# The first two chunks of a linear-attention loop in another order: the second chunk's scores in banks of their own

## The chip, the cores and the metric

The kernel runs on one core of one Trainium2 chip. A core has five engines that each work through their own list of instructions in the written order: TensorE (PE, matrix products; its weight loads are shown apart as PEld), VectorE (DVE), ScalarE (ACT), GpSimd (POOL) and SyncE (SP, which here only issues transfers). They meet through semaphores. PE writes its products to PSUM, a memory of eight banks, and DVE and ACT read them there. The metric is the device time of one launch in microseconds (us), the median of three runs.

## The reference, cut to what matters

The first half is a recurrence over 768 steps for 4 sequences and 8 heads of 48 features; the second sends every token to one of 8 experts.

```
for t in range(S):
    cur = einsum('bhd,bhe->bhde', u * kt, vt)
    y[:, :, t] = einsum('bhd,bhde->bhe', rt, state + cur)
    state = w * state + einsum('bhd,bhe->bhde', kt, vt)
...
expert_idx = argmax(x @ w_gate, axis=1)
...
h = maximum(einsum('ecd,edf->ecf', disp, w1), 0.0)
y = einsum('ecf,efd->ecd', h, w2)
```

## The kernel before, in words

The recurrence is cut into 24 chunks of 128 steps, 6 for each of the 4 sequences. Inside a chunk it becomes matrix products with powers of the decay folded into the keys and queries. Then come routing, scattering of rows by expert, gathering, and the two layers of the experts. The order of everything is written by hand: the tile framework sets waits, and each engine's list follows the program text.

The work of chunk i, by the functions that the change and the prediction name:

- `prep_keys(i)` (L512, DVE) multiplies the loaded tile `dm` by the decay factors `ft`. `product(i)` (L496, on DVE or, by default, POOL) makes `P`, the product of queries and keys of the same step.
- `mix(...)` (L81 and L83, PE) sums two things into one bank `c`: the bonus of a coming chunk out of its `P`, and the gate logits of an earlier chunk out of its output `xs`. `mixed` (L88, ACT) copies that to `ct`; `pull` (L93, PE) turns it, and L94 (DVE) copies the result to `bon` or `l`. `bonus(i)` is pull and copy for the first chunks.
- `diag(i)` (L507, ACT; L505 where half of it is given to DVE) writes the bonus on the diagonal of `s`, eight blocks of 128x128.
- `scores(i)` (L526, PE) makes the products of keys and queries in a PSUM tile `a` of two banks, of which there is one. `masks(i)` (L530, DVE) copies `a` into `s` where the mask allows, so the next scores wait for the mask copy to release `a`.
- `prep_values(i)` (L518, DVE) makes `kt`; `update(i)` (L538, PE) makes the chunk's addition to the state in bank `u`; `state_of(i)` (L545 for the first chunk of a sequence, L548 for the others, DVE) makes the new state `snb`.
- `values1(i)` (L560, PE) and `values2(i)` (L569, PE) sum the output in two banks with the tag `y`: state times queries, then values times `s`. L573 (ACT) copies them to `xs`. `turn` (L105, PE) and `keep_rows` (L111, L112, ACT) turn `xs` into rows for the scatter.
- `setup_keys` (L416 on PE, L417 on ACT) makes `kk` once; its PSUM tile `gp` has the tag `lg`. `warm(n)` (L464) is n matrix products of zeros that nobody reads.

PSUM is full: one bank each for the tags `a1` (the tile `c`), `u`, `xp` and `lg`, two for `y`, two for `a`. The banks of `xp` and `lg` are used later in the loop, by `turn` and by the routing.

Ahead of the loop stand chunk 0's keys, scores and bonus and chunk 1's keys and bonus. Step i of the loop then runs scores(i+1), keys and product of chunk i+3, the mix for chunk i+2, update(i), masks(i+1), pull, turn, state, values of chunk i, diag(i+2). Step 0 and step 1 are written apart from the rest. Loads of `dm` and `bd` run five chunks ahead on SP's queue, with six buffers each.

Of the kernel before, what the change touches and what calls it, by code (L numbers as in the profile page):

```python
# [6 lines left out]
F32 = mybir.dt.float32  # L7
# [14 lines left out]
NP = H // 2  # L22
# [13 lines left out]
def rwkv_moe(nc, tc, dmj, rkv, bdc, wv, wu, uv, wg, w1, w2, out, cap):  # L36
# [4 lines left out]
    with ExitStack() as ctx:  # L41
# [175 lines left out]
        with ExitStack() as mc:  # L217
# [4 lines left out]
            ps1 = mc.enter_context(tc.tile_pool(name="ps1", bufs=1, space=PSUM))  # L222
# [188 lines left out]
                    nc.scalar.mul(out=wd[:, p], in_=idn, mul=w128[:, p:p + 1])  # L411

            def setup_keys(sps):
                gp = sps.tile([128, NP, 128], F32, tag="lg", name="gp")
                for p in range(NP):
                    nc.tensor.matmul(gp[:, p], lhsT=ft[:, p], rhs=wd[:, p], start=True, stop=True)  # L416
                nc.scalar.copy(out=kk.rearrange("q (p h) d -> q p h d", p=NP), in_=gp.rearrange("q p (h d) -> q p h d", h=2)[:, :, :, 0:D])  # L417
# [43 lines left out]
            def warm(n):  # L461
                t = ps1.tile([128, 512], F32, tag="y", name=f"warm{n}", bufs=2)
                for _ in range(n):
                    nc.tensor.matmul(t, lhsT=wz[:, 0:128], rhs=wz, start=True, stop=True)  # L464
# [33 lines left out]
            def diag(i, ps=range(NP), vector=False):  # L498
                t = T[i]
                s = t["s"] = sb[i % 3]  # L500
                for p in ps:
                    for h in range(2):
                        bon = t["bon"][:, 2 * p + h:2 * p + h + 1]
                        if vector:
                            nc.vector.tensor_scalar(out=s[:, h, p], in0=eye, scalar1=bon, scalar2=None, op0=ALU.mult)  # L505
                        else:
                            nc.scalar.mul(out=s[:, h, p], in_=eye, mul=bon)  # L507

            def prep_keys(i):
                dm = T[i]["dm"]  # L510
                n = 64 + D
                nc.vector.tensor_tensor(out=dm[:n], in0=dm[:n], in1=ft[:n].unsqueeze(1).broadcast_to([n, 2, NP, 128]), op=ALU.mult)  # L512
# [6 lines left out]

            def scores(i):  # L520
                t = T[i]
                a = t["a"] = psB.tile([128, 2, NP, 128], F32, tag="a", name=f"a{i}")
                for p in range(NP):
                    for h in range(2):
                        r = slice(64 * h, 64 * h + D)
                        nc.tensor.matmul(a[:, h, p], lhsT=t["dm"][r, 1, p], rhs=t["dm"][r, 0, p], start=True, stop=True)  # L526

            def masks(i):
                t = T[i]
                nc.vector.copy_predicated(t["s"].rearrange("q h p j -> q (h p) j"), msk.unsqueeze(1).broadcast_to([128, 8, 128]),  # L530
                                          t.pop("a").rearrange("q h p j -> q (h p) j"))

# [44 lines left out]
            def bonus(i, c, ct):  # L577
                T[i]["bon"] = sm.tile([128, 2 * E], F32, tag="bon", name=f"bon{i}")
                pull(c, ct, T[i]["bon"])
# [24 lines left out]
            c = mix(T[0]["P"], None, ps1)  # L604
            ct = mixed(c, wk)
            prep_keys(1)
            bonus(0, c, ct)
            diag(0, (0, 1))
            diag(0, (2, 3), True)
            setup_keys(ps1)  # L610
            warm(3)
            product(1, nc.vector)
            c = mix(T[1]["P"], None, ps1)
            masks(0)
            ct = mixed(c, wk)
            warm(2)
            bonus(1, c, ct)
            prep_keys(2)
            product(2, nc.vector)
            diag(1)  # L620
            ws = wstream(0, PLAN0, True)
            for i in range(NI):
                if i + 5 < NI:
                    load(i + 5)
                    load_rows(i + 5)
                if i == 0:
                    values1(0)
                    values2(0)
                    scores(1)
                    c = mix(T[2]["P"], None, ps1)  # L630
                    ct = mixed(c, wk)
                    prep_keys(3)
                    product(3)
                    masks(1)
                    bonus(2, c, ct)
                    warm(3)
                    prep_values(0)
                    prep_values(1)
                    diag(2)
                    next(ws)  # L640
                    continue
                if i == 1:
                    scores(2)
                    update(0)
                    state_of(0)
                    state["s"] = state["next"]
                    prep_values(2)
                if i > 1:
                    each(scores, i + 1)
                each(prep_keys, i + 3)  # L650
                each(product, i + 3)
                if i in (20, 21):
                    gather(0, [i - 20])
                else:
                    scatters(1)
                c = mix(T[i + 2]["P"] if i + 2 < NI else None, T[i - 1]["xs"], ps1)
                ct = mixed(c, wk)
                update(i)
                each(masks, i + 1)
                if i == NI - 1:  # L660
                    pa.close()
                    psA = mc.enter_context(tc.tile_pool(name="psA", bufs=2, space=PSUM))
                    acts = [xtrans(0, j) for j in range(3)]
                if i % NC == NC - 1:
                    xp = turn(i - 1, T[i - 1]["xs"], ps1)
                to = place_of(i - 1, sm, rows_of)
                pull(c, ct, to)
                if i + 2 < NI:
                    T[i + 2]["bon"] = to
                if i % NC < NC - 1:  # L670
                    xp = turn(i - 1, T[i - 1]["xs"], ps1)
                advance()
                next(ws)
                each(prep_values, i + 2)
                if i == NI - 1:
                    take(0)
                    for f in acts:
                        f()
                state_of(i)
                values1(i)  # L680
                each(diag, i + 2, (0, 1, 2))
                values2(i)
                each(diag, i + 2, (3,))
                keep_rows(i - 1, xp, rows_of)
                state["s"] = state.get("next")
                rout(i - 1, sm, ps1, rows_of, "rows")
                advance()
                if i == NI - 1:
                    advance()
                if i == 1:  # L690
                    setup_ok(wc)
                if i == 18:
                    early_places(sm, ps1)
                if i in (9, 13):
                    nc.gpsimd.memset(xg[i == 13], 0.0)
                T.pop(i - 1)
# [303 lines left out]
```

## Time and profile before

| what | before |
|---|---|
| median of 3 runs | 387.28 us (386.78 to 387.33) |
| the profiled execution, its own time | 386.67 us |
| its span, first to last instruction | 385.0 us |
| PE busy | 370.3 us (96%) |
| DVE busy | 236.5 us (61%) |
| ACT busy | 204.4 us (53%) |
| POOL busy | 143.9 us (37%) |

The span leaves out 1.67 us of the profiled execution's own time. The chunks run until about 130 us, the experts after that. A busy share is a mean over both, so a question on the first chunks is answered by the instructions in order of time and by windows, not by this table.

### The profile page before, as it was taken

The numbers are of one execution on the slowest core, as the hardware profiler recorded it, in microseconds if no ns is written. First come the engines' busy times: TensorE is split into PE (matmuls) and PEld (weight loads), VectorE is DVE, ScalarE is ACT, GpSimd is POOL, SyncE is SP. The second block draws the span as 40 slices with busy tenths as digits, with TensorE's granted clock in tenths as the row PEclk, the third lists the DMA queues.
The fourth block names the chain that finished last, engine by engine and source line by source line (L and its number), as shares of the span: only waits on it lengthen the run. The fifth ranks groups of instructions, "written<-read, shape, count | busy, mean of one in ns | idle before, by whom it ended". The sixth has DMA issues, their size and how long they took to land.

```text
span 385.0 us, 9378 instructions
## 1 busy us (share of the span) xinstructions
PE 370.3 (96%) x3569; PEld 335.3 (87%) x3570; DVE 236.5 (61%) x589; ACT 204.4 (53%) x565; POOL 143.9 (37%) x200
## 2 busy tenths in 40 slices
PE   8899999999999997999999999999999999999993
PEld 3677888787787887999999999999999999999992
DVE  6898899999996565736536636536536546543210
ACT  3668898788787532717427517426425525523201
POOL 7124668686662427304403403503502602202203
PEclk9999999999999998999999999999999999999998
DMA  7848868888712544744635535634733743400102
GB/s 296 340 140 289 277 241 286 272 297 263 263 39 79 190 138 130 214 134 132 177 109 163 180 109 137 205 112 120 226 111 115 207 131 113 126 3 17 43 3 72
DMA packets 20950, 62.51 MB, mean 162 GB/s; under 512 B 3996, under 2 KB 4132, under 8 KB 20896
## 3 DMA queue, kind: packets, MB, share of 16 engines
q1 hardware_dynamic: 15120, 46.74, 38.3%
q0 software_dynamic: 5632, 14.56, 11.4%
q8 instruction: 30, 0.49, 0.5%
q10 hardware_dynamic: 144, 0.52, 0.3%
q14 instruction: 24, 0.20, 0.2%
HBM read 52.58 MB, written 10.03 MB: 163 GB/s over the span
## 4 chain that ended last, share of the span: by engine, by line
PE 46%; issue 12%; POOL 2%; DMA 1%; POOLq 1%; ACT 0%; DVE 0%; ACTq 0%
PE a L318 8%; PE a L317 7%; PE a L319 7%; PE b L334 7%; PE b L335 7%; PE b L336 7%; PE yp L350 2%; POOL out L342 2%; PE tp L300 2%; DMA xg<-xsd,pidx 1%; POOLq L757 0%; DMA xsd<-xr,slot 0%; POOLq L933 0%; DVE ws L251 0%; ACT ws L250 0%
## 5 line engine op out<-in xcount | busy, mean ns | idle before, releaser
L342 POOL DMA_INDIRECT out<-yo,ids x32 | 32.4, 1014 | 162.1 <-ACT yo L341 161.1
L317 PE MATMUL a<-xh,ws 128*128 128x416 f32 (+1 forms) x216 | 75.6, 350 | 0.1
L322 ACT ACTIVATE hh<-a 128x416 fp32r<-128x416 f32 (+1 forms) x72 | 34.6, 481 | 76.1 <-PE a L319 70.7
L318 PE MATMUL a<-xl,ws 128*128 128x416 f32 (+1 forms) x216 | 72.8, 337 | 0.0
L319 PE MATMUL a<-xh,ws 128*128 128x416 f32 (+1 forms) x216 | 72.7, 336 | 0.0
L334 PE MATMUL b<-hh,ws 128*128 128x416 f32 (+2 forms) x208 | 71.4, 343 | 0.0
L323 DVE SCALAR_TENSOR_TENSOR hl<-a,hh 128x416 fp32r<-128x416 f32 (+1 forms) x72 | 39.1, 543 | 50.2 <-ACT hh L322 37.2
L336 PE MATMUL b<-hh,ws 128*128 128x416 f32 (+2 forms) x208 | 69.5, 334 | 0.0
L335 PE MATMUL b<-hl,ws 128*128 128x416 f32 (+2 forms) x208 | 69.4, 334 | 0.0
L251 DVE TENSOR_TENSOR ws<-wr,ws 128x384 fp32r<-128x384 f32 (+1 forms) x112 | 67.7, 622 | 0.6
L507 ACT ACTIVATE s<-eye,l 128x128 f32<-128x128 f32 x168 | 53.8, 392 | 15.3 <-DVE l L94 14.7
L250 ACT CAST ws<-wr 128x384 fp32r<-128x384 f32 (+1 forms) x112 | 59.9, 557 | 2.1 <-DMA xsd<-xr,slot 2.1
L337 DVE COPY yt<-b 128x416 f32<-128x416 f32 (+2 forms) x26 | 14.2, 546 | 67.2 <-PE b L336 67.2
L496 POOL TENSOR_TENSOR P<-dm 112x512 f32<-112x512 f32 x21 | 27.1, 1292 | 40.6 <-DVE dm L512 10.9
L317 PEld LDWEIGHTS a<-xh,ws 128*128 128x128 f32 x216 | 41.5, 192 | 0.9 <-DVE xl L305 0.3
L319 PEld LDWEIGHTS a<-xh,ws 128*128 128x128 f32 x216 | 41.5, 192 | 0.4
L318 PEld LDWEIGHTS a<-xl,ws 128*128 128x128 f32 x216 | 41.6, 192 | 0.3 <-DVE xl L305 0.2
L275 POOL DMA_INDIRECT xg<-xsd,pidx x32 | 35.8, 1120 | 14.1 <-issue 12.0
L334 PEld LDWEIGHTS b<-hh,ws 128*128 128x128 f32 x208 | 39.4, 190 | 0.1
L336 PEld LDWEIGHTS b<-hh,ws 128*128 128x128 f32 x208 | 39.2, 188 | 0.3
L335 PEld LDWEIGHTS b<-hl,ws 128*128 128x128 f32 x208 | 39.3, 189 | 0.0
L304 ACT CAST xh<-tp 128x416 fp32r<-128x416 f32 (+1 forms) x27 | 12.3, 472 | 47.3 <-PE tp L300 47.3
(144 smaller groups left out, 573.9 us busy)
## 6 DMA issues: line engine op xcount, KB each, us to landing
wr<-w SPq DMA_DIRECT2D x24, 512.0 KB
wr<-w SPq DMA_DIRECT2D x32, 384.0 KB
dm<-dmj SPq DMA_DIRECT2D x23, 512.0 KB
bd<-bdc SPq DMA_DIRECT2D x24, 384.0 KB
dm<-dmj ACTq DMA_DIRECT2D x1, 512.0 KB
xg<-xsd,pidx POOLq DMA_INDIRECT x32
out<-yo,ids POOLq DMA_INDIRECT x32
xsd<-xr,slot POOLq DMA_INDIRECT x24
```

The source lines that it names most:

```text
L250: nc.scalar.copy(out=hi, in_=r)
L251: low.append(lambda: nc.vector.tensor_tensor(out=lo, in0=r, in1=hi.bitcast(F32), op=ALU.subtract))
L275: nc.gpsimd.indirect_dma_start(out=xg[k % 2][:, i].bitcast(I32), out_offset=None, in_=xsd[:, :], in_offset=bass.IndirectOffsetOnAxis(ap=pi ...
L317: nc.tensor.matmul(a, lhsT=wh, rhs=xh[:, d, o], start=d == 0, stop=False)
L318: nc.tensor.matmul(a, lhsT=wh, rhs=xl[:, d, o], start=False, stop=False)
L319: nc.tensor.matmul(a, lhsT=wl, rhs=xh[:, d, o], start=False, stop=d == 2)
L323: nc.vector.scalar_tensor_tensor(out=hl[:, f, o], in0=a, scalar=0.0, in1=hh[:, f, o].bitcast(F32), op0=ALU.max, op1=ALU.subtract)
L334: nc.tensor.matmul(y, lhsT=wh, rhs=hh[:, f, o], start=f == 0, stop=False)
L335: nc.tensor.matmul(y, lhsT=wh, rhs=hl[:, f, o], start=False, stop=False)
L336: nc.tensor.matmul(y, lhsT=wl, rhs=hh[:, f, o], start=False, stop=f == 7)
L342: r = nc.gpsimd.indirect_dma_start(out=out[:, :], out_offset=bass.IndirectOffsetOnAxis(ap=ids[k][0][:qo, i:i + 1], axis=0), in_=yo, in_off ...
L507: nc.scalar.mul(out=s[:, h, p], in_=eye, mul=bon)
```

## The change

Chunk 1's scores no longer wait for the tile `a`: they go, with the two heads of a pair in different banks, to the two free banks with the tags `xp` and `lg`, straight behind chunk 0's pull. Its mask copy becomes two copies of half the size. `gp` moves to a `y` bank. Chunk 1's product stands ahead of chunk 0's bonus copy; chunk 2's keys stand ahead of chunk 0's mask. The calls of `warm` ahead of the first values are 4 in one call for 3 and 2 before; the 3 in step 0 stay, at another place. Step 0 now also holds update(0), scores(2), the state after chunk 0, and the values of chunk 1, and chunk 3's product is made by DVE and not by POOL. Step 1 leaves out what step 0 has taken over.

```diff
-                gp = sps.tile([128, NP, 128], F32, tag="lg", name="gp")
+                gp = sps.tile([128, NP, 128], F32, tag="y", name="gp", bufs=2)
...
             def scores(i):
                 t = T[i]
-                a = t["a"] = psB.tile([128, 2, NP, 128], F32, tag="a", name=f"a{i}")
+                if i == 1:
+                    a = t["a"] = [ps1.tile([128, NP, 128], F32, tag=n, name=f"a1{n}") for n in ("xp", "lg")]
+                else:
+                    a = t["a"] = psB.tile([128, 2, NP, 128], F32, tag="a", name=f"a{i}")
...
             def masks(i):
                 t = T[i]
+                if i == 1:
+                    for h, a in enumerate(t.pop("a")):
+                        nc.vector.copy_predicated(t["s"][:, h], msk.unsqueeze(1).broadcast_to([128, NP, 128]), a)
+                    return
...
             prep_keys(1)
+            product(1, nc.vector)
             bonus(0, c, ct)
+            scores(1)
             diag(0, (0, 1))
             diag(0, (2, 3), True)
+            c = mix(T[1]["P"], None, ps1)
+            ct = mixed(c, wk)
+            prep_keys(2)
             setup_keys(ps1)
-            warm(3)
-            product(1, nc.vector)
-            c = mix(T[1]["P"], None, ps1)
+            bonus(1, c, ct)
             masks(0)
-            ct = mixed(c, wk)
-            warm(2)
-            bonus(1, c, ct)
-            prep_keys(2)
+            diag(1)
             product(2, nc.vector)
-            diag(1)
+            warm(4)
+            prep_values(0)
...
                 if i == 0:
                     values1(0)
                     values2(0)
-                    scores(1)
+                    update(0)
+                    scores(2)
                     c = mix(T[2]["P"], None, ps1)
                     ct = mixed(c, wk)
+                    masks(1)
+                    state_of(0)
+                    state["s"] = state["next"]
+                    prep_values(1)
+                    warm(3)
+                    bonus(2, c, ct)
                     prep_keys(3)
-                    product(3)
-                    masks(1)
-                    bonus(2, c, ct)
-                    warm(3)
-                    prep_values(0)
-                    prep_values(1)
+                    product(3, nc.vector)
                     diag(2)
+                    values1(1)
+                    values2(1)
+                    prep_values(2)
                     next(ws)
                     continue
-                if i == 1:
-                    scores(2)
-                    update(0)
-                    state_of(0)
-                    state["s"] = state["next"]
-                    prep_values(2)
...
-                values1(i)
+                if i > 1:
+                    values1(i)
                 each(diag, i + 2, (0, 1, 2))
-                values2(i)
+                if i > 1:
+                    values2(i)
```

Below are three places of the engines' lists. A row gives line, operation, output and inputs; in a name the digit behind the letters is the chunk (`dm2` is chunk 2's tile), or for `s` and `snb` the buffer, or for `l` the group of two chunks; the number behind the underscore is the program's own.

DVE's list before, from chunk 1's keys to chunk 2's keys:

```order
L512 TENSOR_TENSOR dm1_115<-dm1_115,ft_128 112x1024
L94 COPY bon0_290<-c_282 128x16
L505 TENSOR_SCALAR s0_120<-eye_131,bon0_290 128x128 x4
L496 TENSOR_TENSOR P1_311<-dm1_115 112x512
L530 COPY_PREDICATED s0_120<-msk_130,a0_273 128x1024
L94 COPY bon1_324<-c_313 128x16
L512 TENSOR_TENSOR dm2_116<-dm2_116,ft_128 112x1024
L496 TENSOR_TENSOR P2_328<-dm2_116 112x512
```

and the same part of the list of the change, on to the first chunk's state:

```order
L496 TENSOR_TENSOR P1_290<-dm1_115 112x512
L94 COPY bon0_292<-c_282 128x16
L505 TENSOR_SCALAR s0_120<-eye_131,bon0_292 128x128 x4
L512 TENSOR_TENSOR dm2_116<-dm2_116,ft_128 112x1024
L94 COPY bon1_327<-c_313 128x16
L537 COPY_PREDICATED s0_120<-msk_130,a0_273 128x1024
L496 TENSOR_TENSOR P2_339<-dm2_116 112x512
L518 TENSOR_TENSOR kt0_346<-bd0_183,kk_129 128x384
L535 COPY_PREDICATED s1_121<-msk_130,a1xp_295 128x512
L535 COPY_PREDICATED s1_121<-msk_130,a1lg_296 128x512
L552 COPY snb0_126<-u_138 128x4x48
```

Chunk 1's product has moved ahead of the first bonus copy, chunk 2's keys ahead of the first mask copy, and the first mask copy behind the second bonus copy.

DVE's list before, from the bonus of chunk 2 to the copy that holds chunk 3's bonus (`l0`):

```order
L94 COPY bon2_382<-c_371 128x16
L518 TENSOR_TENSOR kt0_389<-bd0_183,kk_129 128x384
L518 TENSOR_TENSOR kt1_391<-bd1_185,kk_129 128x384
L545 COPY snb0_126<-u_138 128x4x48
L518 TENSOR_TENSOR kt2_422<-bd2_188,kk_129 128x384
L512 TENSOR_TENSOR dm4_118<-dm4_118,ft_128 112x1024
L530 COPY_PREDICATED s2_122<-msk_130,a2_404 128x1024
L94 COPY l0_447<-c_427 128x16
```

and in the change:

```order
L94 COPY bon2_405<-c_389 128x16
L512 TENSOR_TENSOR dm3_117<-dm3_117,ft_128 112x1024
L496 TENSOR_TENSOR P3_409<-dm3_117 112x512
L518 TENSOR_TENSOR kt2_440<-bd2_188,kk_129 128x384
L512 TENSOR_TENSOR dm4_118<-dm4_118,ft_128 112x1024
L537 COPY_PREDICATED s2_122<-msk_130,a2_380 128x1024
L94 COPY l0_468<-c_448 128x16
```

Two of the three `kt` copies and the state copy have left this stretch to the front; chunk 3's keys and its product, which POOL made before, have come into it.

ACT's list before, from chunk 2's diagonal to the `ct` of chunk 4:

```order
L507 ACTIVATE s2_122<-eye_131,bon2_382 128x128 x8
L88 COPY ct_436<-c_427 128x128
L507 ACTIVATE s0_120<-eye_131,l0_447 128x128 x6
L573 COPY xs1_485<-y1_0_461 128x2x128
L573 COPY xs1_485<-y1_1_462 128x2x128
L507 ACTIVATE s0_120<-eye_131,l0_447 128x128 x2
L111 COPY xr0_123<-idf_70 128x2
L112 COPY xr0_123<-xp0_450 128x384
L88 COPY ct_521<-c_512 128x128
```

and in the change:

```order
L507 ACTIVATE s2_122<-eye_131,bon2_405 128x128 x8
L580 COPY xs1_437<-y1_0_419 128x2x128
L580 COPY xs1_437<-y1_1_420 128x2x128
L88 COPY ct_457<-c_448 128x128
L507 ACTIVATE s0_120<-eye_131,l0_468 128x128 x8
L111 COPY xr0_123<-idf_70 128x2
L112 COPY xr0_123<-xp0_471 128x384
L88 COPY ct_521<-c_512 128x128
```

The two copies of chunk 1's output have moved ahead of chunk 3's diagonal, which before they stood in the middle of.

## Rows read from the trace of the kernel before

**Rows 1.** The profile page: the span, and each engine's busy time.

```profile
span 385.0 us, 9378 instructions
...
PE 370.3 (96%) x3569; PEld 335.3 (87%) x3570; DVE 236.5 (61%) x589; ACT 204.4 (53%) x565; POOL 143.9 (37%) x200
```

**Rows 2.** Windows: stretch, length, busy time of each engine, granted clock, DMA share, GB/s.

```profile
23.10:29.08 5.98, 5.32 (x89) 3.96 (x87) 5.52 (x19) 5.12 (x19) 1.28 (x1) 1.00 0.46 156
29.08:33.81 4.73, 4.73 (x92) 3.89 (x90) 4.52 (x16) 3.77 (x14) 1.64 (x3) 1.00 0.85 283
29.08:119.40 90.32, 89.72 (x1619) 71.97 (x1617) 82.98 (x233) 74.54 (x257) 58.65 (x59) 1.00 0.71 240
143.60:150.42 6.82, 4.78 (x38) 4.06 (x37) 3.96 (x19) 1.30 (x4) 5.60 (x5) 1.00 0.44 132
150.42:153.84 3.42, 3.42 (x18) 3.42 (x18) 2.08 (x4) 1.70 (x4) 2.51 (x4) 0.50 0.34 102
```

**Rows 3.** Timeline of DVE, 8 to 14 us: start, length, instruction, idle before and releaser.

```profile
8.11 1.22 DVE L512 TENSOR_TENSOR dm<-dm,ft 112x1024 f32<-112x1024 f32 x1
10.32 0.17 DVE L94 COPY bon<-c 128x16 f32<-128x16 f32 x1 [0.99 <-PE c L93]
...
11.39 0.69 DVE L496 TENSOR_TENSOR P<-dm 112x512 f32<-112x512 f32 x1
11.99 1.33 DVE L530 COPY_PREDICATED s<-msk,a 128x1024 f32<-128x1024 int32 x1
13.46 0.17 DVE L94 COPY bon<-c 128x16 f32<-128x16 f32 x1
```

**Rows 4.** Timeline of PE, 10 to 15.5 us.

```profile
10.13 1.14 PE L416 MATMUL gp<-wd,ft 128*128 128x128 f32 x8
11.10 0.81 PE L464 MATMUL warm<-wz 128*128 128x512 bf16 x3
12.22 0.42 PE L81 MATMUL c<-P,uwz 112*32 112x128 f32 x8 [0.31 <-DVE P L496]
12.58 0.60 PE L464 MATMUL warm<-wz 128*128 128x512 bf16 x2
13.02 0.40 PE L93 MATMUL c<-pick,ct 128*128 128x16 f32 x2
...
13.95 1.08 PE L569 MATMUL y<-s,bd 128*48 128x128 f32 x16
```

**Rows 5.** Timeline of DVE, 17.7 to 24 us.

```profile
17.77 0.16 DVE L94 COPY bon<-c 128x16 f32<-128x16 f32 x1
...
19.98 0.55 DVE L518 TENSOR_TENSOR kt<-bd,kk 128x384 f32<-128x384 f32 x1
20.44 1.22 DVE L512 TENSOR_TENSOR dm<-dm,ft 112x1024 f32<-112x1024 f32 x1
21.58 1.34 DVE L530 COPY_PREDICATED s<-msk,a 128x1024 f32<-128x1024 int32 x1
22.81 0.16 DVE L94 COPY l<-c 128x16 f32<-128x16 f32 x1
```

**Rows 6.** Timeline of ACT, 13 to 27 us.

```profile
13.66 2.45 ACT L507 ACTIVATE s<-eye,bon 128x128 f32<-128x128 f32 x8 [0.69 <-DVE bon L94]
...
24.78 0.62 ACT L573 COPY xs<-y 128x256 f32<-128x256 f32 x2
25.29 0.70 ACT L507 ACTIVATE s<-eye,l 128x128 f32<-128x128 f32 x2
...
26.34 0.27 ACT L88 COPY ct<-c 128x128 f32<-128x128 f32 x1
```

**Rows 7.** Timeline of PE, 18.5 to 29.5 us.

```profile
19.02 0.56 PE L538 MATMUL u<-bd,kt 128*48 128x48 f32 x16
...
23.10 1.16 PE L526 MATMUL a<-dm 48*128 48x128 f32 x16
24.19 0.41 PE L81 MATMUL c<-P,uwz 112*32 112x128 f32 x2
25.18 0.30 PE L83 MATMUL c<-xs,wgz 128*32 128x128 f32 x1 [0.59 <-ACT xs L573]
...
26.66 0.40 PE L93 MATMUL c<-pick,ct 128*128 128x16 f32 x2
...
29.08 0.60 PE L526 MATMUL a<-dm 48*128 48x128 f32 x6
```

More of the change, by code (lines that the diff above doesn't have):

```diff
@@ L525, in scores @@
                         r = slice(64 * h, 64 * h + D)
-                        nc.tensor.matmul(a[:, h, p], lhsT=t["dm"][r, 1, p], rhs=t["dm"][r, 0, p], start=True, stop=True)
+                        nc.tensor.matmul(a[h][:, p] if i == 1 else a[:, h, p], lhsT=t["dm"][r, 1, p], rhs=t["dm"][r, 0, p], start=True, stop=True)
             def masks(i):
                 t = T[i]
+                if i == 1:
+                    for h, a in enumerate(t.pop("a")):
+                        nc.vector.copy_predicated(t["s"][:, h], msk.unsqueeze(1).broadcast_to([128, NP, 128]), a)
+                    return
                 nc.vector.copy_predicated(t["s"].rearrange("q h p j -> q (h p) j"), msk.unsqueeze(1).broadcast_to([128, 8, 128]),
```

## The prediction

> **What bounds the kernel now.** I read the page first, then windows, then the engines' instructions in order of time up to 30 us; the chain of waits reaches back only into the experts and says nothing of the chunks. The page gives PE 96% of a span of 385.0 us [rows 1]: what counts is when PE waits, not how much the other engines do. By windows, PE waits for nothing once the loop is in step: one whole step is 4.73 of 4.73 us busy, and from 29.08 us, where the scores of chunk 4 begin, to 119.40 us only 0.60 us are missing [rows 2]. The step just before, 23.10 to 29.08, takes 5.98 us and has 0.66 us idle [rows 2]. So everything that the change can move lies ahead of 29.08, and the question is one number: when do the scores of chunk 4 begin afterwards? A shift there goes through, because the loop, the scatter, the gather and the experts each wait for what stands before them.
>
> How rows are added here: the next row of an engine starts a little before the one ahead has ended, 0.07 us on PE (1.16 long, 1.09 apart [rows 7]), 0.08 to 0.11 on DVE [rows 3, 5], 0.11 on ACT [rows 6]. I count from start to start, and the full length where the next one needs the result.
>
> **The change, part by part.**
>
> Chunk 1's product: DVE ends chunk 1's keys at 9.33 and then sits idle 0.99 us until PE has pulled the first bonus [rows 3]. The product's 0.69 fits in there, so the move costs nothing; without that cover it would be 0.60.
>
> Chunk 1's scores, mix and pull: PE is free at 10.13 [rows 4]. Scores take 1.09, to 11.22; the mix follows without the 0.31 us that it waited for the product, 0.38, to 11.60; `gp` takes 0.97 [rows 4], to 12.57. The pull stands there, 0.45 us ahead of its 13.02, since the two calls of `warm` between are gone. The copy of the bonus comes 0.44 behind the pull [rows 3, 4]: 13.01.
>
> The first mask copy: before it starts at 11.99 [rows 3]. Now it is queued behind that bonus copy, so at 13.10, and it ends 1.33 later at 14.43. Chunk 2's keys fill DVE's time ahead of it, so they are off the path. The 4 warm products (0.22 each, by the two that span 12.58 to 13.02 [rows 4]) and the first half of the values bring PE to 14.3, and it waits. The second half of chunk 0's values starts at 14.5, 0.55 later than its 13.95 [rows 4], and takes 1.01, to 15.5. This is the first price of the new order.
>
> Then PE has update(0), which needs `kt` of chunk 0: on DVE 13.10 + 1.23 + 0.60 (product) + 0.55 (`kt` [rows 5]) = 15.48, so about 15.6. Update 0.50 (0.56 less the overlap [rows 7]), scores 1.09, mix 0.38, three warm products 0.66: 18.25 for the pull of chunk 2. From mix to pull by themselves took 0.80 (12.22 to 13.02 [rows 4]), which would be 18.0; so `warm` costs about 0.22 here. The bonus of chunk 2 is copied 0.44 later, at 18.7, against 17.77 [rows 5]: 0.93 later.
>
> The mask copy in two halves: no row has that size. Below, a half costs 0.67, half of 1.33; above, the whole 1.33. I take 0.80, as a DVE operation on 512 elements (0.69) is 0.53 shorter than one on 1024 (1.22) [rows 3]. The halves wait for chunk 1's diagonal on ACT, 0.20 + 2.45 after its bonus [rows 3, 6], so about 15.7, and with state copy and `kt` DVE is done near 17.9. It then waits for the bonus at 18.7: some 0.8 of cover. At 0.80 the split costs nothing, at 1.33 each about 0.3.
>
> From chunk 2's bonus to chunk 3's on DVE: before 22.81 - 17.77 = 5.04 [rows 5]. Now the stretch holds bonus copy 0.09, keys 1.25, product 0.60 (it was POOL's), `kt` 0.46, keys 1.14, mask copy 1.23 [rows 3, 5]: 4.77, without a wait inside. 18.7 + 4.77 = 23.5, against 22.81: 0.7 later. PE has pulled chunk 3's bonus over a microsecond earlier, because values(1) now end near 20.1; it is DVE's list that holds it. POOL loses a job that it did while idle, DVE gains one where DVE is the last.
>
> From chunk 3's bonus to chunk 4's `ct` on ACT: before 26.34 - 22.81 = 3.53, of which the copy of chunk 1's output takes 0.51 (24.78 to 25.29 [rows 6]). That copy now runs ahead of all this, behind chunk 2's diagonal. 23.5 + 3.02 = 26.5, against 26.34. PE's wait of 0.59 us for that copy [rows 7] goes, and a longer one for `ct` takes its place. From the pull at 26.66 to the scores at 29.08 [rows 7] the work is the same and without a gap: +0.2 us.
>
> DVE stays a little further behind than PE: it had 0.25 us of waiting for ACT ahead of the next mask copy, so its 0.7 becomes about 0.4. It fills 4.52 of the next 4.73 us [rows 2], so it makes up at most 0.2 in a step, and PE may come to wait for it once. The sum lies between +0.2 and +0.45; I take +0.35.
>
> The transfers: SP's queue keeps its order; the load into chunk 0's tile waits for the first half of its values, 0.3 later; the next ones are released some 3 us earlier. The DMA engines are at 0.46 there [rows 2] and no instruction of the loop's first steps waits for a load, so neither counts. POOL has one product less.
>
> The sum: 386.67 (the profiled execution's own time, 1.67 outside its span) + 0.35 = 387.02. That execution lies 0.61 below the median of the runs shown, 387.28; against the median the same shift is **387.6 us**. Own range of this case: with `warm` hidden after all +0.0, with the dear halves +0.8.
>
> **The rivals.**
>
> Slower, by the clock: between 20.1 and 26.9 us my sum has PE waiting for chunk 3's product 0.7, for `ct` 0.3, for the mask copy 0.7 and for `ct` again 1.0, together 2.7 of 6.8 us. [...] Against it: 0.66 idle in 5.98 left it at 1.00 [rows 2]. If it falls, 3.42 us at half rate lose at most 1.7 and, as PE has waits to fill, perhaps 0.9: 388.5, up to 389.3. It decides if the waits come as close together as in the sum. [...] 12%.
>
> Slower, ACT gives nothing back: the copy of chunk 1's output needs values(1) done. If these end after about 22 us rather than 20.1, the copy holds up `ct` of chunk 3 and with it the same chain; the 0.51 is lost again: 387.28 + 0.35 + 0.51 = 388.1. Against it: nothing but 2.1 us of PE work stands between the pull at 18.25 and that end. 13%.
>
> Faster: the waits that the change takes away from PE (0.31 for the product [rows 4], 0.59 for the output copy [rows 7], one warm product 0.22) are not replaced: -1.1, 386.2. For that DVE must reach chunk 3's bonus at 22.4 or earlier, over a microsecond sooner than its list of operations adds up to. 13%.
>
> That the change would not do what it says is excluded by the lists: the three scores and two values stand where the words put them.
>
> **How the numbers follow.** Two per mille of the time, 0.77 us, is about what a measurement of this kernel can tell from none. The forecast, +0.35 with +0.0 to +0.8, lies within: 62%. The two slower rivals make 25%, the faster one 13%. The range from 386.5 to 388.8 leaves out most of the faster rival (11%) and the dear end of the clock's (5%).
>
> **What would show it.** Right: chunk 1's scores near 10.1 and done near 11.3; the first mask copy near 13.1; the second half of chunk 0's values near 14.5; chunk 2's bonus copied near 18.7 and chunk 3's near 23.5; values(1) done near 20; two half copies of about 0.8 us; PE waiting for `ct` ahead of a pull near 26.9; scores of chunk 4 near 29.3. Wrong: a granted clock under 1.00 before 30 us; a second wait of PE for ACT in each of the next steps; or the scores of chunk 4 ahead of 29.08, which would mean that DVE was not the one to be waited for.

## The result, and the profile after

The changed kernel took 389.46 us in the median of 15 runs (386.75 to 396.75), the kernel before 386.85 in the same set: ratio 1.0075, 95% interval 1.0054 to 1.0096, so 2.6 us slower. I had forecast 387.6, no difference, range 386.5 to 388.8. The profiled execution of the changed kernel is the longest of the 15, so its total is not taken as the kernel's. From its page, the span and PE's busy share ([rows 1]):

```profile
span 395.1 us, 9368 instructions
...
PE 375.6 (95%) x3568; PEld 340.4 (86%) x3569; DVE 237.1 (60%) x591; ACT 204.5 (52%) x565; POOL 142.5 (36%) x199
```

PE is busy 5.3 us longer than before, with one instruction less.

The runs below came in six sets, A to F, each on one chip, a different one each time. The kernel before runs in every set, and each ratio is to it.

Up to 22.8 us the profile after follows the sum to within 0.3 us. Timeline of DVE in the changed kernel (start, length, instruction, idle before and releaser):

```profile
9.32 0.69 DVE L496 TENSOR_TENSOR P<-dm 112x512 f32<-112x512 f32 x1
12.57 1.33 DVE L537 COPY_PREDICATED s<-msk,a 128x1024 f32<-128x1024 int32 x1
14.91 0.74 DVE L535 COPY_PREDICATED s<-msk,a1xp 128x512 f32<-128x512 int32 x1
15.55 0.71 DVE L535 COPY_PREDICATED s<-msk,a1lg 128x512 f32<-128x512 int32 x1
17.93 0.17 DVE L94 COPY bon<-c 128x16 f32<-128x16 f32 x1 [0.96 <-PE c L93]
22.70 0.17 DVE L94 COPY l<-c 128x16 f32<-128x16 f32 x1
```

Timeline of PE in the same kernel:

```profile
13.96 1.08 PE L576 MATMUL y<-s,bd 128*48 128x128 f32 x16
...
20.02 0.45 PE L81 MATMUL c<-P,uwz 112*32 112x128 f32 x8 [0.52 <-DVE P L496]
...
22.88 2.08 PE L529 MATMUL a<-dm 48*128 48x128 f32 x16 [0.67 <-DVE l L94]
...
31.14 1.23 PE L529 MATMUL a<-dm 48*128 48x128 f32 x8
```

This execution begins its chunks 0.50 us earlier (scores of chunk 0 at 7.48, before at 7.98). With that added, the first mask copy is at 13.07 (13.10 in the sum), the second half of the values at 14.46 (14.5), chunk 2's bonus at 18.43 (18.7) and chunk 3's at 23.20 (23.5). Then the scores of chunk 3, 1.16 long before [rows 7], take 2.08. Windows of the same kernel show the granted clock (columns as in [rows 2]):

```profile
20.00:22.83 2.83, 2.04 (x38) 1.48 (x38) 2.83 (x5) 1.28 (x6) 1.12 (x1) 1.00 0.62 221
22.83:33.07 10.24, 10.19 (x102) 8.31 (x102) 7.36 (x24) 6.73 (x22) 3.04 (x5) 0.50 0.30 89
```

Just before, from 20 to 22.83, PE was busy 2.04 of the 2.83 us, at 1.00; from 22.83 the granted clock stands at 0.50 for 10.24 us. Scores of chunk 4 begin 23.66 us behind those of chunk 0; in the executions below that keep the clock it is 20.96, in the kernel before 21.10. By chunk 12 the gap to one that keeps it is 4.2 us (62.61 against 58.38 in e13_again).

That is one execution. A second thing stands in this trace, far from the change. Timeline of the changed kernel, all engines, near the last chunks:

```profile
117.71 1.08 PE L576 MATMUL y<-s,bd 128*48 128x128 f32 x16
118.08 1.08 POOL L275 DMA_INDIRECT xg<-xsd,pidx  x1 [0.30 <-issue]
119.58 0.65 ACT L580 COPY xs<-y 128x256 f32<-128x256 f32 x2 [0.77 <-PE y L576]
...
124.13 1.01 POOL L173 DMA_INDIRECT xsd<-xr,slot  x1 [0.31 <-issue]
125.64 0.65 ACT L580 COPY xs<-y 128x256 f32<-128x256 f32 x2 [1.48 <-PE a L529]
```

ACT's copies of the output stand idle 0.77 and 1.48 us, though PE ended what they need at 118.79 and 123.95. The kernel before has neither.

### The profile page after: what moved, and what is told of

It is laid out like the page before. It is cut to its first block, busy times and chain, and to the rows that moved or that the text cites. A ratio compares the mean times of both kernels' runs of the same rounds, so it can differ in the third digit from the quotient of the medians.

```text
span 395.1 us, 9368 instructions
## 1 busy us (share of the span) xinstructions
PE 375.6 (95%) x3568; PEld 340.4 (86%) x3569; DVE 237.1 (60%) x591; ACT 204.5 (52%) x565; POOL 142.5 (36%) x199
## 4 chain that ended last, share of the span: by engine, by line
PE 70%; issue 13%; DVE 6%; ACT 6%; POOL 2%; DMA 1%; another core or an unknown queue 1%; POOLq 1%; DVEq 0%; ACTq 0%
PE a L319 8%; PE a L317 8%; PE a L318 8%; PE b L334 7%; PE b L335 7%; PE b L336 7%; PE a L529 5%; PE y L576 5%; ACT s L507 3%; PE y L567 3%; PE xp L105 2%; PE yp L350 2%; PE tp L300 2%; POOL out L342 2%; PE c L93 2%
## 5 line engine op out<-in xcount | busy, mean ns | idle before, releaser
L496 POOL TENSOR_TENSOR P<-dm 112x512 f32<-112x512 f32 x20 | 25.8, 1289 | 44.4 <-DVE dm L512 14.9
L275 POOL DMA_INDIRECT xg<-xsd,pidx x32 | 34.6, 1081 | 14.0 <-issue 11.8
L537 DVE COPY_PREDICATED s<-msk,a 128x1024 f32<-128x1024 int32 x23 | 31.1, 1353 | 10.8 <-ACT s L507 7.4
```

The lines of the kernel that those rows point to most:

```text
L275: nc.gpsimd.indirect_dma_start(out=xg[k % 2][:, i].bitcast(I32), out_offset=None, in_=xsd[:, :], in_offset=bass.IndirectOffsetOnAxis(ap=pi ...
```

## The experiments

**Set A: is it the clock, or the order?** All with the change but for the last.

e1_again, the change unaltered. 

> The changed kernel once more, unaltered, for a profile of an ordinary execution. Clock theory: the scores of chunk 4 would stand near 29.3 us at full clock, and most executions show a mean granted clock of 0.988 or less instead of 0.992, with a stretch at 0.50 between 20 and 35 us that costs 1 to 2 us (one stretch of about 3.4 us) or more; median 388 to 390. Chain theory (the new order is later by itself, through DVE and ACT): the scores of chunk 4 come 2 us later than 29.08 in executions whose clock stays at 1.00 as well, and time does not go with the mean clock.

384.78 us, before 385.18: ratio 0.9972 (0.9943 to 1.0002). No loss on this chip. Two of 12 executions have a mean granted clock of 0.974 and took 389.1 and 389.19, 4.3 and 4.4 above the median: about the price seen in the trace after. The clock theory's 388 to 390 did not come. The profiled execution keeps its clock, though PE did the same in it: counted from chunk 0's scores it was busy 6.54 of the 7.83 us that end where the clock fell in the trace after, and 6.55 there. Windows of e1_again:

```profile
22.83:33.07 10.24, 8.96 (x169) 7.34 (x171) 9.93 (x34) 7.77 (x28) 3.38 (x5) 1.00 0.47 148
```

Its scores of chunk 4 begin 20.96 us behind those of chunk 0 (21.10 before), which is against the chain theory too; those of chunk 20 97.31 (97.37), of chunk 21 102.30 (102.07), of chunk 23 111.64 (111.42). So the new order gains a little over twenty chunks and loses 0.28 us in one step, far from the edit. Timeline of the kernel before, PE and ACT:

```profile
106.68 0.42 PE L83 MATMUL c<-xs,wgz 128*32 128x128 f32 x8
107.26 0.27 ACT L88 COPY ct<-c 128x128 f32<-128x128 f32 x1 [0.28 <-PE c L83]
```

Timeline of e1_again, the same instructions:

```profile
106.47 0.42 PE L83 MATMUL c<-xs,wgz 128*32 128x128 f32 x8
107.32 0.27 ACT L88 COPY ct<-c 128x128 f32<-128x128 f32 x1 [0.56 <-PE c L83]
107.64 0.40 PE L93 MATMUL c<-pick,ct 128*128 128x16 f32 x2 [0.25 <-ACT ct L88]
```

ACT's copy starts 0.16 us behind the end of the mixing products before, and 0.43 behind it here, and PE waits. ACT's wait is 0.56 in the trace after and in e15_all and 0.55 in e18_all too, and 0.28 or 0.29 in e14_scatter, e16_blater and e17_scatter, variants of the kernel before. GpSimd issues no transfer there; what holds the copy is open.

e2_fill, products of zeros in PE's early waits:

```diff
+            def fill(n):
+                t = ps1.tile([128, 512], F32, tag="lg", name=f"fill{n}")
+                for _ in range(n):
+                    nc.tensor.matmul(t, lhsT=wz[:, 0:128], rhs=wz, start=True, stop=True)
```

> The changed kernel with ten products of zeros put into PE's waits: 2 ahead of the mix of chunk 3, 1 and 4 ahead of the pulls of chunks 3 and 4, 3 ahead of the scores of chunk 3, 0.22 us each, into a bank that nobody uses then. Nothing else is altered. Clock theory: the granted clock stays at 1.00 up to 120 us and the time falls to 387.0 to 387.8, the +0.3 of the order alone. Chain theory: the time stays at 389 or rises by up to 1 us, since PE gets more to do.

385.69, ratio 1.0006 (0.9977 to 1.0035), lowest mean clock 0.988. It was not faster than e1_again; only the executions at 0.974 are absent.

e3_pool, chunk 3's product back on GpSimd:

```diff
-                    product(3, nc.vector)
+                    product(3)
```

> The changed kernel with the product of chunk 3 on POOL, as it was before the change, not on DVE. Chain theory: DVE reaches the bonus of chunk 3 about 0.6 us earlier, and the time falls by 0.6 at least. Clock theory: PE waits longer for that product (1.27 instead of 0.69 us) but shorter for the mask copy and for ct, so the waits stay about as close together, the clock still falls in many executions, and the median stays over 388.

386.35, ratio 1.0044 (1.0012 to 1.0076). Scores of chunk 4 come 0.36 later than in e1_again, not earlier, counted from those of chunk 0 (21.32 against 20.96). So the product on DVE is not what is dear. Neither theory's time came. Four of 12 executions had a mean clock of 0.982 or lower.

e4_nowarm, the kernel before without eight `warm` products among its first steps:

```diff
-            warm(3)
...
-            warm(2)
...
-                    warm(3)
```

> The kernel before without the three calls of warm for 3, 2 and 3 products of zeros ahead of the first values and in step 0; the order is that of before. Clock theory: no instruction that counts comes later (0 to 0.3 us earlier), but PE has 1.8 us less to do between 11 and 18 us, and if the clock falls it is slower by 1 to 2 us in those executions. Chain theory: the same time as before or up to 0.3 us faster.

386.73, ratio 1.0040 (1.0015 to 1.0065); 10 of 12 executions at a mean of 0.983 or lower, and the profile shows 0.50 from 13.61 to 17.02 us, where the kernel before shows 1.00. Windows of e4_nowarm:

```profile
13.61:17.02 3.41, 3.41 (x38) 2.73 (x32) 2.84 (x3) 2.89 (x10) 0.39 (x1) 0.50 1.05 410
```

After set A I held the clock for the whole cause.

**Set B: the clock, again.** e5_again, the change unaltered. 

> The change unaltered, once more, beside the three others. Clock theory: where the mean granted clock of an execution is that of one of before, its time is within 0.5 us of before's; what lies above it comes from executions whose mean clock is 0.984 or below, so the ratio follows their share: 0.997 to 1.001 if they are 2 in 12 as last time, 1.006 to 1.009 if they are 8 in 12. Order theory (the new order itself costs the 2.6 us): executions at the same mean clock as before's are 2 us or more longer, whatever their share.

388.54, before 386.92: ratio 1.0047 (1.0022 to 1.0071), with only 2 of 12 executions at 0.984 or lower. At equal clocks it is slower too: three executions at 0.988 have the median 388.22, five of the kernel before 387.30; at 0.992, 387.67 (one execution) against 386.24. The clock is not all.

e6_both, the fill of e2_fill and zero products in PE's two waits for gathered rows; e7_gather, the second part alone on the kernel before (for these the tile of zeros is kept to the end):

```diff
                 for i in range(m):
+                    if (k, j) == (1, 0):
+                        gfill(3 + i)
                     nc.tensor.transpose(out=tp[:, q * i:q * i + q], in_=xg[k % 2][:, i, 128 * j:128 * j + 128],
```

> The change with the zero products of e2_fill in the early waits, and with 3 and 4 more in TensorE's two waits for the gathered rows near 144 and 146 us. Clock theory: no half-clock stretch before the tail, mean clock 0.994 or 0.995 in nearly all executions, median 1.5 to 3 us below the kernel before and below the change alone: ratio 0.992 to 0.997. Order theory: no change against e5_again, 1.000 and above.

388.33, ratio 1.0047 (1.0013 to 1.0082), with 9 of 12 executions at 0.994 or above. The clock was repaired and the time was not.

> The kernel before with only the 3 and 4 zero products in the waits for the gathered rows. Clock theory: the stretch at 0.50 near 147 to 154 us (3.4 us, worth 1.7) is gone, mean clock 0.994 or above, ratio 0.993 to 0.997. If that stretch does not hang on TensorE's waits there, it stays and the ratio is 1.000.

386.83, ratio 1.0004 (0.9976 to 1.0031), 11 of 12 at 0.994 or above. The stretch at 0.50 behind the gather [rows 2] is gone, and its 1.7 us are lost elsewhere: from 150 to 160 us PE is now idle 2.3 us, waiting for DVE's `hl` behind late ACT copies, where before it was busy all the time at a granted 0.83. Windows of e7_gather:

```profile
150.00:160.00 10.00, 7.71 (x66) 7.33 (x66) 5.40 (x12) 5.27 (x14) 6.06 (x6) 1.00 0.52 149
```

e8_thin, the change without its own seven `warm` products:

```diff
-            warm(4)
...
-                    warm(3)
```

> The change without its seven products of zeros (four after the second bonus, three ahead of the third). Clock theory: an early stretch at 0.50 in most executions, mean clock 0.984 or below, 1.5 to 5 us above the executions of e5_again that keep the clock, ratio 1.003 to 1.012. Order theory: the products cost their 0.2 us each where TensorE waits for nothing, so 0 to 0.4 us faster than e5_again.

388.82, ratio 1.0055 (1.0028 to 1.0082), but not by the way that I named: no execution below 0.986, and no early fall in the profile, with PE idle 2.21 of 10 us. Nor was it faster than e5_again. Windows of e8_thin:

```profile
20.00:30.00 10.00, 7.79 (x142) 6.18 (x140) 9.72 (x28) 7.31 (x27) 2.54 (x2) 1.00 0.41 124
```

So the theory that too little early work makes the fall does not stand as put.

**What sets B from A.** Comparing the two traces of the same program, e1_again and e5_again, ACT's waits for PE differ at 85.5, 115.7 and 121.5 us. Timeline of e1_again, all engines:

```profile
84.10 1.27 POOL L173 DMA_INDIRECT xsd<-xr,slot  x1 [0.16 <-issue]
84.96 0.61 ACT L580 COPY xs<-y 128x256 f32<-128x256 f32 x2
85.08 0.33 SPq L490 DMA_DIRECT2D bd<-bdc  x1
...
114.12 1.08 POOL L275 DMA_INDIRECT xg<-xsd,pidx  x1 [0.30 <-issue]
114.75 0.62 ACT L580 COPY xs<-y 128x256 f32<-128x256 f32 x2
```

Timeline of e5_again, the first of these places:

```profile
84.15 1.27 POOL L173 DMA_INDIRECT xsd<-xr,slot  x1 [0.16 <-issue]
85.53 0.33 SPq L490 DMA_DIRECT2D bd<-bdc  x1
85.53 0.65 ACT L580 COPY xs<-y 128x256 f32<-128x256 f32 x2 [0.44 <-PE y L576]
```

On B's chip the copy and SP's load, which both wait for PE's last value product, start together at 85.53, 0.11 us behind the end of GpSimd's indirect transfer (84.15 + 1.27). On A's chip they don't wait for it. So the theory, called that of the late copy below: on some chips what waits for PE does not start while GpSimd issues such a transfer. That a signal of PE is not seen then is my guess at the reason; no trace shows it. Both kernels have the wait at 85.5 (0.47 in the trace before, 0.44 in e5_again); I take it as the mark of such a chip. In the kernel before, the second gather runs from 114.65 to 115.73, its copy starts at 114.69 and is not held. Counted from PE's value products, the changed kernel has DVE's keys of chunk 23 0.3 earlier and GpSimd's gather 0.6; it runs from 114.16 in e5_again, and the copy starts at 115.66. Other such transfers run across the ends of values too, at 89.65 and 99.40 in the trace before, and no copy waits: ACT was still at other work and came to its copies only behind them, at 91.19 and 100.94. SP's loads there, which wait for the same products, are against the theory: they start at 90.24 and 99.86, inside the transfers and 0.14 and 0.05 us behind the end of the values. Rival: ACT's own stream of instructions stalls there, whatever GpSimd does.

**Sets C and D: move GpSimd alone.** e9_later and e12_later, the change with two clears of a dead tile ahead of the second gather:

```diff
                 if i in (20, 21):
+                    if i == 21:
+                        for _ in range(2):
+                            nc.gpsimd.memset(wd, 0.0)
                     gather(0, [i - 20])
```

> The change, with two clears of a dead tile (about 1 us of GpSimd) ahead of its second early gather, which runs from 114.16 to 115.24 us in e5_again. Theory of the late copy (where ScalarE's copy of the values shows 0.44 us of waiting at 85.5, as in e5_again, a signal from TensorE is not seen while GpSimd issues an indirect transfer): the gather now starts at 115.1, behind the end of the values at 114.87, so the copy at 115.66 starts at 114.9 or earlier and its 0.77 us wait is gone; the scatter that stands from 120.02 to 121.03 moves too, so the 1.33 us ahead of the next copy shrink or go; scores of the last chunk at 119.4 to 119.5 instead of 119.96, and the time 0.5 to 1.2 us below that of e11_again. Rival (ScalarE's own stream stalls at these instructions, whatever GpSimd does): the waits of 0.77 and 1.33 stay where they are, time that of e11_again. Where the chip shows no wait at 85.5, as in e1_again, both expect no wait at 115 and no difference to e11_again.

C's chip shows no wait at 85.5. 385.55, ratio 1.0016 (0.9990 to 1.0043): nothing told.

e10_blater, the kernel before with three clears there. 

> The kernel before, with three such clears (1.4 us) ahead of the same gather, which there runs from 114.65 to 115.73 and so behind the end of the values. Theory of the late copy: the gather now runs from 116.05 to 117.1, across the end of the mixing products at 116.45; ScalarE's copy of the mixing result, 116.61 in the kernel before, starts at 117.1 to 117.6, the pull behind it too, and the time rises by 0.3 to 1.0 us, if the chip is one with the wait at 85.5. Rival (ScalarE's own stream): the copy stays at 116.6 and the time that of the kernel before.

384.95, ratio 0.9984 (0.9957 to 1.0010), on the same chip: nothing told.

> The change unaltered beside these two. If the profile shows the 0.44 us wait at 85.5, it shows those of 0.77 and 1.33 at 115.7 and 121.5 too and the ratio is 1.003 to 1.009; if not, 0.997 to 1.002.

385.39, ratio 1.0020 (0.9991 to 1.0049), no waits at 85.5, 115 or 121; one execution at 0.974 took 389.51.

Set D came to a chip with the wait. 

> The same as e9_later, in the hope of a chip with the 0.44 us wait at 85.5. If it is there: theory of the late copy, no wait of ScalarE at 115.7 (0.77 in e5_again) and a smaller one or none at 121.5 (1.33), scores of the last chunk at 119.4 to 119.6, time 0.5 to 1.2 us below e13_again; rival (ScalarE's own stream), both waits stay and so does the time. If it is not there: no waits in either, times equal within 0.5 us.

> The change unaltered beside it: with the wait at 85.5 also those at 115.7 and 121.5, and 1.003 to 1.009; without it 0.997 to 1.003, what is above 1.000 from executions whose early clock falls.

e13_again (unaltered): 389.41, ratio 1.0043 (1.0010 to 1.0076), no execution below 0.986. e12_later: 388.47, ratio 1.0038 (1.0003 to 1.0073), three executions at 0.986 or lower among its 12. At 0.988 the medians are 389.57 (7 executions) and 388.45 (5). Timeline of e13_again, all engines:

```profile
113.68 1.08 PE L576 MATMUL y<-s,bd 128*48 128x128 f32 x16
114.06 1.08 POOL L275 DMA_INDIRECT xg<-xsd,pidx  x1 [0.31 <-issue]
115.54 0.65 ACT L580 COPY xs<-y 128x256 f32<-128x256 f32 x2 [0.76 <-PE y L576]
...
118.83 1.08 PE L576 MATMUL y<-s,bd 128*48 128x128 f32 x16
119.91 1.01 POOL L173 DMA_INDIRECT xsd<-xr,slot  x1 [0.30 <-issue]
121.39 0.65 ACT L580 COPY xs<-y 128x256 f32<-128x256 f32 x2 [1.26 <-PE a L529]
```

Timeline of e12_later, the same stretch:

```profile
113.74 1.13 POOL L662 MEMSET wd<- 128x512 f32 x2
114.69 0.62 ACT L580 COPY xs<-y 128x256 f32<-128x256 f32 x2
115.15 1.09 POOL L275 DMA_INDIRECT xg<-xsd,pidx  x1 [0.28 <-issue]
...
118.41 1.08 PE L576 MATMUL y<-s,bd 128*48 128x128 f32 x16
119.13 1.04 POOL L173 DMA_INDIRECT xsd<-xr,slot  x1 [2.37 <-DMA xg<-xsd,pidx]
119.48 0.62 ACT L580 COPY xs<-y 128x256 f32<-128x256 f32 x2
120.47 1.01 POOL L173 DMA_INDIRECT xsd<-xr,slot  x1 [0.30 <-ACT xs L580]
```

ACT's program is the same and both waits are gone, though GpSimd does more work. The first rows of the experts start 0.94 us sooner (125.79 against 126.73, both kernels with chunk 0's scores at 7.63), and the medians differ by 0.94. The ratios to the kernel before, 1.0043 and 1.0038, do not tell the two runs apart within their intervals; e12_later has more executions with a low clock. The rival falls by the trace. Not told apart is whether GpSimd's instruction holds the copy or the transfer that it issues, since both moved. What is left is one wait of 0.89 at 122.05 ahead of ACT's next copy, which the kernel before has too (0.78).

**Sets E and F: the same rule in the kernel before, and both cures together.** e14_scatter and e17_scatter, the kernel before with its last such scatter moved off the mixing products:

```diff
                 else:
+                    if i == 23:
+                        for _ in range(4):
+                            nc.gpsimd.memset(wd, 0.0)
                     scatters(1)
```

> The kernel before, with four clears of a dead tile (2 us of GpSimd) ahead of the scatter that runs there from 120.25 to 121.26 us, across the end of the last mixing products (120.9). Theory of the late copy, if the chip shows the wait at 85.5: ScalarE's 0.78 us ahead of the copy at 121.9 goes, TensorE's 0.28 and 0.32 behind it too, and the time falls by 0.4 to 0.8 us: ratio 0.998 to 0.999. Rival (ScalarE's own stream): wait and time stay. Without the wait at 85.5 both expect no change.

E's chip has no wait at 85.5: 385.23, ratio 0.9993 (0.9965 to 1.0021).

> The same as e14_scatter, in the hope of a chip with the wait at 85.5: if it is there, no wait ahead of ScalarE's copy near 121.9 (0.78 in the kernel before) and 0.4 to 0.8 us less, ratio 0.998 to 0.999; rival, the wait stays and so does the time. If it is not there: no change.

F's chip has it: 387.62, before 388.62, ratio 0.9967 (0.9934 to 1.0000). Timeline of the kernel before:

```profile
120.25 1.01 POOL L173 DMA_INDIRECT xsd<-xr,slot  x1 [0.30 <-ACT xs L573]
120.49 0.43 PE L83 MATMUL c<-xs,wgz 128*32 128x128 f32 x8
121.92 0.27 ACT L88 COPY ct<-c 128x128 f32<-128x128 f32 x1 [0.78 <-PE c L83]
122.24 0.40 PE L93 MATMUL c<-pick,ct 128*128 128x16 f32 x2 [0.32 <-ACT ct L88]
```

Timeline of e17_scatter, the same stretch:

```profile
120.35 2.29 POOL L657 MEMSET wd<- 128x512 f32 x4
120.56 0.43 PE L83 MATMUL c<-xs,wgz 128*32 128x128 f32 x8
121.11 0.27 ACT L88 COPY ct<-c 128x128 f32<-128x128 f32 x1
121.43 0.40 PE L93 MATMUL c<-pick,ct 128*128 128x16 f32 x2
```

ACT's copy starts 0.8 us sooner, as the theory says, and PE's pull with it. The experts' first rows come 116.82 us behind chunk 0's scores, 117.68 in the trace before: 0.86. The 1.0 us in the medians is a little more than the 0.4 to 0.8 expected, and the interval reaches to no difference.

e15_all and e18_all, the change with both delays and the ten early zero products. 

> The change with both delays on GpSimd (two clears ahead of the second early gather, four ahead of that scatter) and the ten early zero products of e2_fill. If both causes hold and nothing else does, it is 1.2 to 1.8 us faster than the change alone on a chip with the wait at 85.5, has no execution of mean clock below 0.984, and stands within 0.4 us of the kernel before: ratio 0.999 to 1.001. Without that wait: 0.999 to 1.001 too, since only the clock is left.

385.47, ratio 0.9998 (0.9972 to 1.0024), lowest mean clock 0.987.

> The same as e15_all: on a chip with the wait at 85.5, ratio to the kernel before 0.999 to 1.001, where the change alone had 1.004 to 1.008, and no execution whose clock falls early (none of mean clock 0.975); more than 1.002 would leave a third cause open. If the wait is not there: 0.999 to 1.001 as well.

387.27, ratio 0.9973 (0.9938 to 1.0008): no loss against the kernel before. The change unaltered did not run on F's chip, so how much of a loss went is not shown there; and the moved scatter cures the kernel before too, so the fair partner is e17_scatter, at 387.62. One execution of 391.89 had a mean of 0.983; one of 513.87 at 0.655, and one of the kernel before in set B (451.4 at 0.754), stand apart and are not explained. The moved scatter made a new late copy of its own, 0.5 us, where it met the next values. Timeline of e18_all:

```profile
122.90 1.08 PE L581 MATMUL y<-s,bd 128*48 128x128 f32 x16
122.92 1.15 POOL L173 DMA_INDIRECT xsd<-xr,slot  x1 [0.30 <-issue]
124.39 0.65 ACT L585 COPY xs<-y 128x256 f32<-128x256 f32 x2 [2.13 <-PE y L581]
```

e16_blater, as e10_blater. 

> The same as e10_blater (the kernel before, its gather laid across the end of the mixing products at 116.45), in the hope of a chip with the wait at 85.5. If it is there: theory of the late copy, ScalarE's copy at 116.6 starts at 117.1 to 117.7 and the time rises by 0.3 to 1.0 us, less what the moved scatter gives back at 121.9; rival, the copy stays and so does the time.

Set E again, no wait at 85.5: 385.31, ratio 0.9984 (0.9958 to 1.0010). So a late copy was never laid into the kernel before on purpose on a chip that shows them.

e17_scatter and e18_all can't be told apart by time. The simpler of the two is e17_scatter, which is the kernel before with four clears, not the change: 1.0 us faster than the kernel before by the medians where the late copies occur, equal where they don't.

## Why the prediction was wrong

**The sum of the order: near in size, by luck.** +0.35 was forecast. On the three chips without the late copies the experts' first rows come 117.02 to 117.03 us behind chunk 0's scores with the change (e1_again, e9_later, e11_again, e15_all), 116.75 to 116.81 in the variants of the kernel before (e10_blater, e14_scatter, e16_blater), which differ from it in nothing ahead of 114 us: +0.25. But that is not the shift that was added up. The half mask copies took 0.74 and 0.71 (0.80 taken). Counted as above, chunk 2's bonus is at 18.43 in e1_again (18.7 in the sum), and what follows took what was forecast: 4.80 us to chunk 3's bonus (4.77), 2.98 to `ct` (3.02). PE waited where named: 0.52 for the product, 0.67 for the mask copy, 0.90 for `ct` (0.7, 0.7 and 1.0 in the sum). So the term that was mis-sized is the 0.93 by which chunk 2's bonus was to be late, measured 0.66, and the scores of chunk 4 came 0.14 earlier instead of 0.2 later, one of the prediction's own signs of being wrong. DVE's lag cost nothing in the steps behind: the change is still 0.06 ahead at chunk 20, and the +0.25 comes from the one wait at 107.3, which no term names.

**The step that failed first: "A shift there goes through".** I took everything behind 29.08 us as a row that only moves. The wait at 107.3 is against that on chips of both kinds (0.56 us in e1_again, 0.55 in e18_all). And GpSimd and PE are two rows, and the change shifted one against the other by some 0.6 us. Eighty-five microseconds behind the edit, gather and scatter then lay across the ends of PE's values. On D's chip, which shows it, moving the gather gives back 0.94 us (e12_later against e13_again, by trace and by median). All late copies together delay the experts' first rows by 2.07 us in the change (119.10 in e13_again against 117.03) and by 0.86 in the kernel before (117.68 against 116.82 in e17_scatter): 1.2 more in the change. No rival of mine named it, and the row that could have warned stood in the trace before: the wait of 0.78 at 121.92, with the scatter at 120.25 ahead of it. I had read that stretch only through PE's 0.60 us of idle time in 90 [rows 2].

**The step that failed second: the clock's rival, in its size.** I gave it the length of the one stretch at 0.50 in the trace before, 3.42 us [rows 2], which lose 0.9 to 1.7 us, and 12%. In the trace after the stretch is 10.24 us and costs 4.2; executions at a mean of 0.974 or 0.975 stand 3.8 to 4.4 us above the median of their run (e1_again, e11_again, e12_later). A mean of 0.984 or lower had 12 of 63 executions of the change unaltered (7 of 15 in the first set), 3 of the kernel before's 174 with a recorded clock, 2 of 48 with the fills. So the fall was named as a risk and its price was too low by a factor of two and a half to five; its share swings between sets.

The first set's 2.6 us are then, as an estimate, 0.25 for the wait at 107.3 and 1.2 for the late copies in each execution, and 0.55 for the executions whose clock fell early: the eight at 0.986 or higher have the median 388.9. Some 0.6 is left. In set D, too, e13_again's median stands 2.35 above the kernel before's without an early fall, where its trace and the trace before give 1.42 up to the experts' first rows. Part of that may be the stretch at 0.50 behind the gather, 6.83 us in e13_again's profile and in the trace after, 3.42 in the trace before; no run tests it.

What stays open: why the same program loses the clock in some executions and keeps it in others, and more often in the first set; e8_thin shows that PE's early waits alone don't decide (idle 2.21 of 10 us at a granted 1.00), and e1_again's profile that the same work of PE can go either way. The executions of e1_again have mean clocks from 0.974 to 0.995; no run here shows what sets them apart.

The rival "ACT gives nothing back" did not come: chunk 1's output copy stood at 20.50, ahead of `ct` at 21.02. The faster rival came nowhere.

## What to carry to other kernels

A change that leaves every engine's own list alone behind a point can still cost there, since it shifts the lists against one another (GpSimd's against PE's by 0.6 us here), and a sum that ends at that point can come out near the total by luck. So follow the shift to the end, step by step, look in the trace before for waits whose releaser had long been done, and ask what else ran at that moment. Before settling on a cause, time the unaltered change on another chip: by set A alone the clock looked like the whole cause, and set B contradicted it. Where GpSimd issues indirect transfers, try them away from the ends of products that another engine waits for: on a chip with the late copies, two clears on GpSimd (1.13 us) ahead of one gather took ACT's waits of 0.76 and 1.26 us away and brought the experts' first rows 0.94 us forward (e12_later against e13_again); on C's chip, which has none, they gained nothing (385.55 against 385.39). Such a dummy operation is a cheap test.

## What the hardware showed that I had not expected

On the chips of sets B, D, F and the first, several instructions that wait for PE (ACT copies, an SP load) start 0.1 to 0.7 us behind the end of the GpSimd indirect transfer that runs when PE is done: 85.53 behind 85.42 (e5_again), 115.54 behind 115.14 and 121.39 behind 120.92 (e13_again), 121.92 behind 121.26 (before). On those of A, C and E the same instructions overlap and nothing waits: the copy starts at 84.96 in e1_again and at 84.64 in e14_scatter, inside the transfers from 84.10 and 83.78. The kernel before is slower on the former as well: 386.85 to 388.62 against 384.90 to 385.44. Not every overlap holds the copy: the scatters at 119.13 (e12_later), 118.91 (before) and 123.26 (e17_scatter), which start after GpSimd stood idle for 2.37, 2.66 and 0.62 us, did not; those that did start within 0.31 us of the instruction ahead of them. Nor does every such close one hold what waits: SP's loads at 90.24 and 99.86 (before) started inside the transfers from 89.65 and 99.40, which had stood behind idle times of 0.15 and 0.16. Why, and why only some chips, is open.

Keeping the clock gained nothing in e7_gather (ratio 1.0004): a stretch at a granted 0.50 was taken away on B's chip, and PE was idle 2.3 us between 150 and 160 us instead. That is not so everywhere. On A's chip the kernel before's own executions at a mean clock of 0.995 took 382.0 to 382.3 us and those at 0.992 took 383.9 to 384.1, where on B's chip the medians at 0.996 to 0.998 and at 0.992 are 386.0 and 386.24. No run put the fill of e7_gather on a chip without the late copies.
